# Four tiles of the first expert, ranked after six of nine attention blocks and multiplied in the stretch between attention and the first expert loop

## The chip, the cores and the metric

One Trainium2 chip; the program runs on one of its cores. TensorE (PE, with its weight loads PEld), VectorE (DVE), ScalarE (ACT), GpSimd (POOL) and SyncE (SP, which issues most DMAs) each run their own list of instructions in order and wait for one another through semaphores. The metric is the device time of one execution in microseconds; lower is better. A clock throttle grants TensorE 1.2 or 2.4 GHz; the profile gives it as a share of 2.4 (0.50 or 1.00).

## The reference

Three layers. Attention over q, k, v of shape (4, 8, 576, 64), with keys and values averaged over groups of 8. Its output, as x of 2304 rows by 512, goes through a mixture of 8 experts that takes the best expert alone, and then through a second layer in which every row goes through every expert, with Sinkhorn weights.

```python
logits = x @ w_gate                      # layer 1
e_idx = np.argmax(logits, axis=1)
for e in range(E):
    mask = e_idx == e
    h = np.maximum(x[mask] @ w1[e], 0.0)
    out[mask] = gate_w[mask, None] * eom[mask, e, None] * (h @ w2[e])
...
for e in range(E):                       # layer 2: all rows, all experts
    out += P[:, e:e + 1] * (np.maximum(x @ w1[e], 0.0) @ w2[e])
```

With the inputs of the reference, 1217 of the 2304 rows go to expert 0, 571 to expert 3, 28 to 4, 348 to 6, 140 to 7, none to the others. Of the 1536 rows of attention blocks 0 to 5, 571 go to expert 0. Both counts come from computing the reference.

## The kernel before

Matmuls are done in float16 with each operand split into a high and a low half, three products per pair (`PASSES`). A tile is 128 rows.

**Attention** (`attention`, L387) goes through nine blocks of 256 rows in the order 0 to 5, 8, 6, 7. A block has transposes of q, scores and exponentials (two halves), transposes of the exponentials, the weighing by values (`weigh`, which also gives the gate logits), and a write of the rows to the DRAM tensor `rowd`. `top1` (L468) picks the experts of finished blocks; the last call handles block 7. Meanwhile `between` loads expert 0's weights, and splits them into halves.

**Routing** (`route`, L488) needs the choices of all rows: matmuls with `ones16` count rows per expert, matmuls with `prior` and `tri` give each row its rank in the order of experts, DVE and POOL turn ranks into one-hot tiles, a matmul of these gives `idx`, the row numbers in the order of experts. POOL then issues one indirect DMA per tile of 128 sorted rows (`gather`, L798) from `rowd` into one of 8 buffers in `raw2`. `columns` (L819) transposes a gathered tile on TensorE; ACT and DVE write its halves to `xT`. `stages` and `coefs1` make the table of experts and the coefficients.

All of this up to the product of sorted tile 0 (`one`, L833: 96 matmuls of 128 columns with w1, relu and split, 24 matmuls of 512 columns with w2) is recorded by `Notes` (L1183), a planner. It lists each engine's instructions by simulating the engines with estimated costs: of what is ready on an engine, the one with the lowest number in program order goes first, `late` being added to that number. The order that it writes is fixed; on the chip an engine that reaches an instruction whose input is late waits, and everything behind it waits too.

**The expert loop** (`moe1`, L881) follows, in code with run-time branches (`tc.If` on register values). Tiles 1 to 8 of expert 0 run one by one; after each, one of the eight pieces of the next expert's weights is split (`step`). The columns of the last eight gathered tiles come after tiles 1 and 2. Then tile 9, and the other experts in turn (`item`), each splitting the weights of the expert after it during its own first two tiles. POOL meanwhile prepares weights of layer 2 (`ahead`, L964), from the moment the gather buffers are free. Layer 2 fills the rest of the span.

Of the kernel before, what the change touches and what calls it, by code (L numbers as in the profile page):

```python
# [20 lines left out]
P = 128  # L21
# [359 lines left out]

LATE = {"scores": -50, "weigh": 150, "key_layout": 100}


def attention(g):  # L387
# [282 lines left out]
def stages(g):  # L670
# [43 lines left out]
    )  # L714
    stg = g.tile([P, 5, E], F32, "stg")
    nc.vector.tensor_reduce(stg, pick, axis=AX.X, op=ALU.add)
    nc.vector.tensor_copy(g.stgi, stg[:, 0:3])
    cm = g.tile([P, 2, E, NT], F32, "cm")

    def bc(r):  # L720
# [72 lines left out]


GB = 8


def gather(g, j):  # L798

    gr = g.gat[:, j % GB]  # L800
    g.nc.gpsimd.indirect_dma_start(
        out=gr,
        out_offset=None,
        in_=g.rowd,
        in_offset=bass.IndirectOffsetOnAxis(ap=g.idx[:, j:j + 1], axis=0),
        bounds_check=N - 1,
        oob_is_err=False,
    )
    g.rows[j] = gr


def gathered(g, first, last):
    for j in range(first, last):
        columns(g, j, g.rows.pop(j))
        if j + GB < NT:
            gather(g, j + GB)


def columns(g, j, gr):  # L819
# [8 lines left out]
    hi, lo = [g.xT[:, s, :, j * P:(j + 1) * P] for s in range(2)]  # L828
    nc.scalar.copy(hi, pt)
    nc.vector.tensor_tensor(lo, pt, hi, op=ALU.subtract)  # L830

# [49 lines left out]
def moe1(g, first):  # L881
# [9 lines left out]
    xts = []
    for i in range(4):
        xt = g.xt.tile([P, 2, KC, P], F16, name=f"xt{i}")
        xts.append(xt)
# [1236 lines left out]
def attention_moe_moe(ctx: ExitStack, tc, q, k, v, wg, wo, w1, w2, wgb, w1b, w2b, out):  # L2131
# [50 lines left out]
    g.stgi = g.per.tile([P, 3, E], I32, name="stgi")  # L2182
# [141 lines left out]
```

## Time and profile before

| | |
|---|---|
| median of 3 runs | 1770.49 us (1770.3 to 1773.25) |
| profiled execution | 1781.27 us, span 1779.5 us |
| mean granted clock | 0.979 |
| PE / DVE / ACT / POOL busy in the span | 95% / 70% / 59% / 16% |
| last weighing of attention ends on PE | 119.2 us |
| first matmul of the expert loop | 162.97 us |
| first matmul of expert 3 | 262.43 us |

A busy share is an average over the stages; what a change inside one stage does is read from the instructions and waits of that stage. In the rows below, the first number of a timeline row is its start in us from the start of the span, the second its length. The helper that records instructions gives nearly all of the first 163 us the line L1293.

### The profile page before, as it was taken

What the parts mean: (1) busy time and instruction counts of PE and PEld (TensorE: products, weight loads), DVE (VectorE), ACT (ScalarE), POOL (GpSimd) and SP (SyncE); (2) the same over time, 40 slices, a digit from 0 to 9 for tenths busy, and PEclk for the clock granted to TensorE, in tenths of its full rate; (3) what the DMA queues carried; (4) which work ended last, traced back from release to release, by engine and by line L of the source; (5) the groups of instructions that cost most, each with busy time, mean ns of one, the idle gap of its engine ahead of it and who ended that gap; (6) DMA issues with size and microseconds to landing.
All of it is one profiled execution on the core that took longest, in us unless ns stands there. A gap on an engine that the chain in (4) does not pass through costs nothing. (4 is left out here: it accounts for less than half of the span.)

```text
span 1779.5 us, 40062 instructions
## 1 busy us (share of the span) xinstructions
PE 1698.0 (95%) x17079; PEld 1482.7 (83%) x17079; DVE 1239.6 (70%) x2218; ACT 1049.1 (59%) x1916; POOL 285.7 (16%) x300
## 2 busy tenths in 40 slices
PE   5868999997999999999999999999999999999997
PEld 4756776676898889889888988898899889888986
DVE  7884436667896785787588567856876786597663
ACT  4743333454577775776577557756766775576542
POOL 7833678400000000000000000000000000000011
PEclk9988999998899999999999999999999999999999
DMA  9625345357331242244134313422441242234211
GB/s 302 161 64 175 108 144 167 134 166 303 105 134 45 87 151 37 39 113 112 25 83 114 78 25 76 132 56 37 113 125 25 60 130 74 36 72 123 104 54 42
DMA packets 83170, 183.86 MB, mean 103 GB/s; under 512 B 27664, under 2 KB 35856, under 8 KB 81168
## 3 DMA queue, kind: packets, MB, share of 16 engines
q1 hardware_dynamic: 68912, 131.66, 22.3%
q0 software_dynamic: 14048, 49.29, 13.2%
q8 instruction: 145, 2.38, 0.5%
q14 instruction: 65, 0.53, 0.1%
HBM read 121.16 MB, written 59.77 MB: 102 GB/s over the span
## 5 line engine op out<-in xcount | busy, mean ns | idle before, releaser
L1797 PEld LDWEIGHTS <-w1c 128*128 128x128 f16 x6720 | 604.3, 98 | 64.6 <-issue 2.2
L1896 PEld LDWEIGHTS <-hs 128*128 128x128 f16 x6048 | 590.6, 98 | 69.8 <-issue 1.9
L1797 PE MATMUL ua<-xc,w1c 128*128 128x256 f16 (+1 forms) x3840 | 426.7, 262 | 0.8 <-DVE xc L1460 0.6
L1896 PE MATMUL da<-x,hs 128*128 128x256 f16 x2592 | 318.2, 273 | 1.4 <-ACT z L1434 0.9
L1959 POOL DMA_DIRECT2D sums<-x x54 | 45.9, 850 | 1243.8 <-ACT x L1436 1208.8
L1797 PE MATMUL uc<-xc,w1c 128*128 128x256 f16 (+1 forms) x1920 | 214.1, 263 | 0.7 <-DVE xc L1460 0.5
L1817 DVE TENSOR_TENSOR u<-u,uc 128x512 f32<-128x512 f32 x144 | 98.7, 685 | 76.6 <-ACT u L1434 61.9
L1817 DVE TENSOR_TENSOR p<-p,ub 128x512 f32<-128x512 f32 x72 | 49.3, 685 | 140.8 <-PE ub L1797 140.8
L1434 ACT COPY u<-ua 128x512 f32<-128x512 f32 x144 | 83.7, 582 | 88.3 <-PE ua L1797 87.9
L1460 DVE TENSOR_TENSOR hs<-h,hs 128x512 f16<-128x512 f32 x144 | 98.8, 686 | 43.2 <-ACT hs L1434 43.2
L1460 DVE TENSOR_TENSOR hs<-u,hs 128x512 f16<-128x512 f32 x144 | 98.9, 687 | 39.2 <-ACT hs L1434 39.2
L1436 ACT ACTIVATE u<-u 128x512 f32<-128x512 f32 x144 | 90.9, 632 | 38.6 <-DVE u L1817 38.5
L858 ACT ACTIVATE wa<-ph 128x512 f32<-128x512 f32 x42 | 25.1, 597 | 139.1 <-PE ph L853 102.8
L1797 PE MATMUL ub<-xc,w1c 128*128 128x256 f16 (+1 forms) x960 | 106.3, 262 | 0.0
L1896 PE MATMUL da<-w2r,hs 128*128 128x256 f16 x864 | 106.1, 273 | 0.0
L1896 PE MATMUL db<-x,hs 128*128 128x256 f16 x864 | 106.1, 273 | 0.0
L1896 PE MATMUL dc<-x,hs 128*128 128x256 f16 x864 | 106.1, 273 | 0.0
L1896 PE MATMUL dc<-w2r,hs 128*128 128x256 f16 x864 | 106.1, 273 | 0.0
L1434 ACT CAST hs<-p 128x512 f16<-128x512 f32 x144 | 89.3, 620 | 26.4 <-DVE p L1460 26.1
L1460 DVE TENSOR_TENSOR hs<-p,hs 128x512 f16<-128x512 f32 x144 | 98.5, 684 | 0.6 <-ACT hs L1434 0.6
L868 PEld LDWEIGHTS <-wa 128*128 128x128 f16 x504 | 48.5, 99 | 60.5 <-DVE wa L860 5.8
L1436 ACT ACTIVATE p<-p 128x512 f32<-128x512 f32 x72 | 45.2, 628 | 86.3 <-DVE p L1817 86.3
(271 smaller groups left out, 2598.4 us busy)
## 6 DMA issues: line engine op xcount, KB each, us to landing
raw<-in_moe_w_dram SPq DMA_DIRECT2D x56, 512.0 KB, 4.0
wr<-in_moe_w_dram SPq DMA_DIRECT2D x54, 512.0 KB, 4.5
sums<-x POOLq DMA_DIRECT2D x54, 512.0 KB
xc<-cspill SPq DMA_DIRECT2D x14, 1792.0 KB, 7.2
cspill<-xc SPq DMA_DIRECT2D x8, 896.0 KB, 4.4
sums<-x SPq DMA_DIRECT2D x9, 512.0 KB, 3.3
x<-sums SPq DMA_DIRECT2D x9, 512.0 KB, 3.7
wa<-in_k_dram SPq DMA_DIRECT2D x4, 1024.0 KB, 10.3
```

The source lines that it names most:

```text
L858: nc.scalar.activation(hr[:, sl], ph, AF.Relu, scale=HSC)
L868: nc.tensor.matmul(py, hs[:, a, k, :], w.w2[:, b, k, :], start=(k == 0 and t == 0), stop=(k == FC - 1 and t == 2),)
L1434: self.nc.scalar.copy(o, x)
L1436: self.nc.scalar.activation(o, x, func, scale=scale)
L1460: lambda: e.tensor_tensor(o, x, y, op=op), reads, writes, late,
L1797: nc.tensor.matmul(o, g.w1c[:, l, a, k, f * P:(f + 1) * P], g.xc[:, pr, r, b, k, :], start=(first and fi == 0 and n == 0), stop=(n == 5), ...
L1817: lambda: nc_.tensor_tensor(o_[0], o_[0], x_[0], op=ALU.add),
L1896: nc.tensor.matmul(t[x][0][:, lo], g.hs[:, sl[f // 2], l, a, f % 2, :], g.w2c[r][:, b, f, :], start=(first and n == 0), stop=(n == 11), sk ...
L1959: lambda: nc.gpsimd.dma_start(sums, x, accum_op=ALU.add), xk, [sk],
```

## The change

After block 5, `top1` is called for columns 8 to 12 too, and a new function `early_rows` ranks the rows of blocks 0 to 5 that go to expert 0. It gathers the first four tiles (512 rows) of them into the raw weight buffers wr2 and wr3. As sorted order takes rows block by block, these are sorted tiles 0 to 3, provided that at least 512 rows were found; `full` says so for each tile. `early_tiles` records the transposes and products of the four tiles with `late` at 300 and not before the last block's transposes of exponentials; their results, without coefficients, go back into wr2 and wr3 until `early_out` multiplies them by `cm`. Tile 4 takes the place that tile 0 had at the end of the planned part. The gathers run in the order 4 to 17, 0 to 3. The loop has tiles 5 to 8, with two weight pieces split after each, and the last eight gathered tiles after tiles 5 and 6. Then a new branch, over a register loaded from a fourth row of `stgi`, computes again those of tiles 0 to 3 that were not full; with these inputs it is skipped. Weights of later experts use the raw buffers shifted by two. At the start, zeros are written to 128 rows of `rowd` that the early gathers may name in their bounds.

```diff
-LATE = {"scores": -50, "weigh": 150, "key_layout": 100}
+LATE = {"scores": -50, "weigh": 150, "key_layout": 100, "early_rows": 250}
...
+    none = g.tile([64, DM], F32, "none")
+    nc.gpsimd.memset(none, 0.0)
+    for b in range(EB // 2 - 1):
+        nc.sync.dma_start(g.rowd[b * S + 512:(b + 1) * S, :], none)
...
             put(exp_transpose, ex, eT, tail)
+        g.spread = len(g.notes.tasks) - 1
...
-        if n in (3, 8, 6, 7):
-            put(top1, *{3: (0, 8), 8: (16, 18), 6: (8, 14), 7: (14, 16)}[n])
+        if n in (3, 5, 8, 6, 7):
+            put(top1, *{3: (0, 8), 5: (8, 12), 8: (16, 18), 6: (12, 14), 7: (14, 16)}[n])
+        if n == 5:
+            put(early_rows)
...
     def raw(self, i):
-        return self.g.wr[(8 * self.stage + i) % RAW]
+        return self.g.wr[(8 * self.stage + 2 * (self.stage > 0) + i) % RAW]
...
+NE = 4
+EB = 6
+ORDER = [*range(NE, NT), *range(NE)]
...
+def early_rows(g):
+    nc = g.nc
+    T = 2 * EB
+    oh = g.oh[:, 0, 0:T]
+    pc = bank2(g)
+    nc.tensor.matmul(pc[0:T, 0, 0:P], oh, g.ones16, start=True, stop=True)
+    nc.scalar.copy(cnt, pc[0:T, 0, 0:P])
+    nc.tensor.matmul(rk, cnt, g.prior[0:T, 0, 0:T + 1], start=True, stop=False)
...
+    nc.tensor.matmul(rk, g.tri, ohx, start=False, stop=True)
...
+    for t in range(T):
+        ohp = new([P, P], BF16, "eohp", 3)
+        nc.vector.tensor_scalar(
+            ohp, g.iof16, lof[:, 0, t:t + 1], 1.0, op0=ALU.is_equal, op1=ALU.mult
+        )
+        nc.tensor.matmul(
+            px[:, 0, 0:2 * NE], ohp, ohv[:, t].rearrange("p x j -> p (x j)"),
+            start=(t == 0), stop=(t == T - 1),
+        )
...
+    nc.vector.tensor_tensor(idx, high, px[:, 0, NE:2 * NE], op=ALU.add)
+    for c in range(NE):
+        gather_rows(g, g.early[c], idx[:, c:c + 1], EB // 2 * S - 64)
+
+def early_tiles(g, w):
+    for c in range(NE):
+        columns(g, g.early[c], g.xts[c])
+    for c in range(NE):
+        product(g, w, g.xts[c], lambda py, c=c: g.nc.scalar.copy(g.early[c], py), c)
+
+def early_out(g):
+    nc.vector.tensor_tensor(ce, g.cm[:, 0, 0:NE], g.full, op=ALU.mult)
+    for c in range(NE):
+        nc.vector.tensor_scalar(g.x2[:, c], g.early[c], ce[:, c:c + 1], None, op0=ALU.mult)
+        nc.vector.tensor_reduce(
+            g.am2[:, c:c + 1], g.x2[:, c], axis=AX.X, op=ALU.max, apply_absolute_value=True
+        )
...
-    for c in range(1, 9):
+    for c in range(NE + 1, 9):
         first_tiles(c)
-        if c < 3:
-            gathered(g, NT - GB * (3 - c) // 2, NT - GB * (2 - c) // 2)
-        w[1].step(c - 1)
+        i = c - NE - 1
+        if i < 2:
+            gathered(g, NT - GB * (2 - i) // 2, NT - GB * (1 - i) // 2)
+        w[1].step(2 * i, 2 * i + 1)
+    with tc.If(g.s_a[NE] > 0):
+        for c in range(NE):
+            with tc.If(g.s_a[c] > 0):
+                one(
+                    g, first, g.xT[:, :, :, c * P:(c + 1) * P], slice(c, c + 1),
+                    g.cm[:, 0, c:c + 1],
+                )
...
         attention(g)
+        g.notes.late, g.notes.after = 300, g.spread
+        early_tiles(g, first)
+        g.notes.late, g.notes.after = 0, None
...
         route(g)
...
+        early_out(g)
         gathered(g, 0, NT - GB)
-        one(g, first, g.xT[:, :, :, 0:P], slice(0, 1), g.cm[:, 0, 0:1])
+        one(
+            g, first, g.xT[:, :, :, NE * P:(NE + 1) * P], slice(NE, NE + 1),
+            g.cm[:, 0, NE:NE + 1],
+        )
```

`product` is `one` without the coefficient: the same 96 and 24 matmuls, always with the same hidden buffer, and an ACT copy of the result.

PE's instructions behind the last weighing of block 7 (`xT,x`, 81 columns), where the routing's count (`ones,oh`) and ranks (`prior,wb`) follow; before:

```order
L1293 MATMUL ab_274<-xT,x_97 128x81
L1293 LDWEIGHTS oh
L1293 MATMUL ab_277<-ones_115,oh 128x128
...
L1293 MATMUL ab_277<-ones_115,oh 16x128
L1293 LDWEIGHTS wb
L1293 MATMUL ab_275<-prior,wb 128x144
```

The same place in the changed kernel (`wr` holds the early rows, `xt_171` their columns; the lines left out are 60 matmuls with `xt_171` ahead of the count, and 24 between count and ranks):

```order
L1446 MATMUL ab_296<-xT,x_97 128x81
L1446 MATMUL ab_294<-ident,wr_71 128x128 x4
L1446 MATMUL ab_293<-ident,wr_71 128x128 x4
L1446 MATMUL ab_295<-ident,wr_72 128x128 x4
L1446 MATMUL ab_294<-ident,wr_72 128x128 x4
...
L1446 MATMUL ab_296<-xt_171,wa 128x128
L1446 LDWEIGHTS oh
L1446 MATMUL ab_293<-ones_115,oh 128x128
...
L1446 MATMUL ab_296<-xt_171,wa 128x128
L1446 LDWEIGHTS wb
L1446 MATMUL ab_295<-prior,wb 128x144
```

All 16 transposes of early rows and five eighths of the first early product with w1 now stand ahead of the count.

DVE's instructions at the last block's gate logits (`lgt`) and expert choice (`mx`, `eq`, `fi`, `oh`), on which the count waits; before:

```order
L1293 TENSOR_TENSOR raw_98<-ab_274,wa 128x640
L1293 TENSOR_REDUCE lgt<-raw_98 128x32
L1293 TENSOR_REDUCE mx<-lgt 128x2
L1293 TENSOR_TENSOR eq<-lgt,mx 128x16
L1293 TENSOR_TENSOR eq<-eq,rev 128x16
L1293 TENSOR_REDUCE fi<-eq 128x2
L1293 TENSOR_TENSOR oh<-fi,rev 128x8x2
```

And in the changed kernel:

```order
L1446 TENSOR_TENSOR xt_171<-ab_294,xt_171 128x512
...
L1446 TENSOR_TENSOR raw_98<-ab_296,wa 128x640
...
L1446 TENSOR_TENSOR xt_172<-ab_293,xt_172 128x512
L1446 TENSOR_REDUCE lgt<-raw_98 128x32
L1446 TENSOR_TENSOR xt_173<-ab_295,xt_173 128x512
L1446 TENSOR_REDUCE mx<-lgt 128x2
L1446 TENSOR_TENSOR xt_174<-ab_294,xt_174 128x512
L1446 TENSOR_TENSOR eq<-lgt,mx 128x16
L1446 TENSOR_TENSOR eq<-eq,rev 128x16
L1446 TENSOR_REDUCE fi<-eq 128x2
L1446 TENSOR_TENSOR oh<-fi,rev 128x8x2
```

The low halves of the four early tiles have been put between the last block's logits and its expert choice.

## Rows read from the trace of the kernel before

**Rows 1.** Windows: length; busy us (instructions) of PE, PEld, DVE, ACT, POOL; PEclk, DMA, GB/s.
```profile
98.00:120.00 22.00, 18.84 (x352) 16.25 (x351) 19.52 (x46) 11.54 (x13) 0.95 (x1) 0.92 0.33 74
119.00:163.00 44.00, 25.44 (x207) 18.63 (x207) 26.44 (x111) 12.55 (x19) 22.73 (x22) 0.73 0.47 155
```

**Rows 2.** Timeline of PE: start, length, what; idle before it, and its releaser.
```profile
114.62 4.55 PE L1293 MATMUL ab<-xT,x 128*128 128x81 f16 x70 [1.02 <-DVE x L1293]
122.19 0.49 PE L1293 MATMUL ab<-ones,oh 128*128 128x128 bf16 x2 [3.01 <-DVE oh L1293]
123.62 0.56 PE L1293 MATMUL ab<-prior,wb 128*128 128x144 bf16 x2
128.15 2.14 PE L1293 MATMUL ab<-wb 128*128 128x36 bf16 x18 [3.97 <-POOL wb L1293]
134.65 1.11 PE L1293 MATMUL ab<-ident,raw 128*128 128x128 f32 x4 [4.36 <-DMA raw<-rowd,idx]
138.57 2.76 PE L1293 MATMUL ab<-xT,wa 128*128 128x128 f16 x24
162.97 5.52 PE L853 MATMUL ph<-xT,wa 128*128 128x128 f16 x96 [0.94 <-DVE x L1293]
168.33 5.34 PE L868 MATMUL py<-wa 128*128 128x512 f16 x24
173.51 1.91 PE L827 MATMUL py<-ident,raw 128*128 128x128 f32 x16
```

**Rows 3.** Timeline of DVE, end of attention and routing.
```profile
112.53 0.82 DVE L1293 TENSOR_TENSOR x<-ab,wa 128x640 f32<-128x640 f32 x1
114.98 0.41 DVE L1293 SCALAR_TENSOR_TENSOR x<-ab,x 64x256 f16<-64x256 f32 x1
121.95 0.17 DVE L1293 TENSOR_TENSOR oh<-fi,rev 128x16 bf16<-128x16 f32 x1
126.11 3.91 DVE L1293 TENSOR_SCALAR wb<-iof,wb 128x128 bf16<-128x128 bf16 x16
130.54 0.17 DVE L1293 TENSOR_TENSOR idx<-wb,ab 128x18 int32<-128x18 f32 x1
136.47 0.69 DVE L1293 TENSOR_TENSOR xT<-ab,xT 128x512 f16<-128x512 f32 x1 [2.91 <-ACT xT L1293]
```

**Rows 4.** Timeline of POOL: first and fourth gather, first and last DMA of `ahead`.
```profile
131.01 1.27 POOL L1293 DMA_INDIRECT raw<-rowd,idx  x1 [1.82 <-DVE wb L1293]
135.20 1.00 POOL L1293 DMA_INDIRECT raw<-rowd,idx  x1 [0.30 <-issue]
188.01 0.58 POOL L976 DMA_DIRECT2D raw<-in_moe_w_dram  x1 [28.65 <-PE py L827]
334.95 0.68 POOL L1006 DMA_DIRECT2D w2spill<-raw  x1 [0.30 <-POOL raw L1002]
```

**Rows 5.** Windows with the granted clock (PEclk, third from the end).
```profile
138.00:141.00 3.00, 3.00 (x27) 2.93 (x26) 2.56 (x10) 0.58 (x1) 2.39 (x3) 0.50 0.61 193
141.00:144.00 3.00, 2.77 (x31) 2.56 (x29) 0.00 (x0) 0.00 (x0) 2.39 (x3) 0.79 0.65 203
```

**Rows 6.** Waits from 100 to 165 us: total, times, longest.
```profile
DVE xT L1293 <- issue: 6.7, 1, 6.7
PE ab L1293 <- issue: 3.6, 4, 2.5
```

**Rows 7.** Timeline of PE and DVE in the expert loop.
```profile
262.43 5.52 PE L853 MATMUL ph<-xt,wb 128*128 128x128 f16 x96 [0.94 <-DVE x L873]
270.73 8.14 DVE L785 SCALAR_TENSOR_TENSOR wa<-wr,wa 128x1024 f16<-128x1024 f32 x4
282.65 6.36 PE L868 MATMUL py<-wb,wa 128*128 128x512 f16 x22 [3.67 <-DVE wa L860]
346.51 7.16 PE L853 MATMUL ph<-xt,wb 128*128 128x128 f16 x96 [2.35 <-PEq L925]
355.94 4.63 DVE L785 SCALAR_TENSOR_TENSOR wa<-wr,wa 128x1024 f16<-128x1024 f32 x4 [0.27 <-ACT wa L784]
```

More of the change, by code (lines that the diff above doesn't have):

```diff
@@ L716, in stages @@
     nc.vector.tensor_reduce(stg, pick, axis=AX.X, op=ALU.add)
-    nc.vector.tensor_copy(g.stgi, stg[:, 0:3])
+    nc.vector.tensor_copy(g.stgi[:, 0:3], stg[:, 0:3])
+    again = g.tile([P, 2, E], F32, "again")
+    nc.vector.memset(again, 0.0)
+    nc.vector.tensor_scalar(
+        again[:, 1, 0:NE], g.iof[:, 0:NE], stg[:, 1, 0:1], None, op0=ALU.is_lt
+    )
+    nc.vector.tensor_scalar(
+        again[:, 0, 0:NE], g.full, -1.0, 1.0, op0=ALU.mult, op1=ALU.add
+    )
+    nc.vector.tensor_tensor(
+        again[:, 0, 0:NE], again[:, 0, 0:NE], again[:, 1, 0:NE], op=ALU.mult
+    )
+    nc.vector.tensor_reduce(
+        again[:, 0, NE:NE + 1], again[:, 0, 0:NE], axis=AX.X, op=ALU.add
+    )
+    nc.vector.tensor_copy(g.stgi[:, 3], again[:, 0])
     cm = g.tile([P, 2, E, NT], F32, "cm")
@@ L737, in registers @@
         min_val=0, max_val=NT,
+    )
+    _, g.s_a = nc.values_load_multi_w_load_instructions(
+        tab[:, 3 * E:3 * E + NE + 1], engines=[ET.PE, ET.DVE, ET.Activation, ET.SP],
+        min_val=0, max_val=NE,
     )
@@ L795, with gather_rows @@
 GB = 8
-def gather(g, j):
-    gr = g.gat[:, j % GB]
+NE = 4
+EB = 6
+ORDER = [*range(NE, NT), *range(NE)]
+def gather_rows(g, gr, idx, n=N):
     g.nc.gpsimd.indirect_dma_start(
@@ L803, in gather @@
         out_offset=None,
-        in_=g.rowd,
-        in_offset=bass.IndirectOffsetOnAxis(ap=g.idx[:, j:j + 1], axis=0),
-        bounds_check=N - 1,
+        in_=g.rowd[0:n, :],
+        in_offset=bass.IndirectOffsetOnAxis(ap=idx, axis=0),
+        bounds_check=n - 1,
         oob_is_err=False,
     )
+def gather(g, i):
+    gr = g.gat[:, i % GB]
+    j = ORDER[i]
+    gather_rows(g, gr, g.idx[:, j:j + 1])
     g.rows[j] = gr
 def gathered(g, first, last):
[L813 to L816, printed above, removed]
@@ L819, in columns @@
-def columns(g, j, gr):
+    for i in range(first, last):
+        j = ORDER[i]
+        columns(g, g.rows.pop(j), g.xT[:, :, :, j * P:(j + 1) * P])
+        if i + GB < NT:
+            gather(g, i + GB)
+def early_rows(g):
+    nc = g.nc
+    new = g.tile
+    T = 2 * EB
+    oh = g.oh[:, 0, 0:T]
+    pc = bank2(g)
+    nc.tensor.matmul(pc[0:T, 0, 0:P], oh, g.ones16, start=True, stop=True)
+    cnt = new([T, P], BF16, "ecnt")
+    nc.scalar.copy(cnt, pc[0:T, 0, 0:P])
+    rk = pc[:, 1, 0:T + 1]
+    nc.tensor.matmul(rk, cnt, g.prior[0:T, 0, 0:T + 1], start=True, stop=False)
+    ohx = new([P, T + 1], BF16, "eoh")
+    nc.vector.memset(ohx[:, T:T + 1], 0.0)
+    nc.vector.tensor_copy(ohx[:, 0:T], oh)
+    nc.tensor.matmul(rk, g.tri, ohx, start=False, stop=True)
+    full = new([P, 1], F32, "en")
+    nc.vector.tensor_copy(full, rk[:, T:T + 1])
+    nc.vector.tensor_scalar(g.full, g.iof[:, 0:NE], -float(P), full, op0=ALU.mult, op1=ALU.add)
+    nc.vector.tensor_scalar(g.full, g.full, float(P), None, op0=ALU.is_ge)
+    off = new([P, T], F32, "eoff")
+    nc.vector.tensor_scalar(off, oh, 8192.0, -8192.0, op0=ALU.mult, op1=ALU.add)
+    nc.vector.tensor_tensor(off, off, rk[:, 0:T], op=ALU.add)
+    posi, ints = new([P, T], I32, "eposi"), new([P, 2, T], I32, "eints")
+    nc.vector.tensor_copy(posi, off)
+    nc.vector.tensor_scalar(ints[:, 0], posi, 127, None, op0=ALU.bitwise_and)
+    nc.vector.tensor_scalar(ints[:, 1], posi, 7, None, op0=ALU.arith_shift_right)
+    lof = new([P, 2, T], F32, "elof")
+    nc.vector.tensor_copy(lof, ints)
+    ohj, ohv = new([P, T, NE], BF16, "eohj"), new([P, T, 2, NE], BF16, "eohv")
+    nc.vector.tensor_tensor(
+        ohj, g.iof[:, 0:NE].unsqueeze(1).to_broadcast([P, T, NE]),
+        lof[:, 1].unsqueeze(2).to_broadcast([P, T, NE]), op=ALU.is_equal,
+    )
+    nc.vector.tensor_tensor(
+        ohv, ohj.unsqueeze(2).to_broadcast([P, T, 2, NE]),
+        g.tok[:, 0:T].unsqueeze(3).to_broadcast([P, T, 2, NE]), op=ALU.mult,
+    )
+    px = bank2(g)
+    g.notes.whole = False
+    for t in range(T):
+        ohp = new([P, P], BF16, "eohp", 3)
+        nc.vector.tensor_scalar(
+            ohp, g.iof16, lof[:, 0, t:t + 1], 1.0, op0=ALU.is_equal, op1=ALU.mult
+        )
+        nc.tensor.matmul(
+            px[:, 0, 0:2 * NE], ohp, ohv[:, t].rearrange("p x j -> p (x j)"),
+            start=(t == 0), stop=(t == T - 1),
+        )
+    g.notes.whole = True
+    high, idx = new([P, NE], F32, "ehigh"), new([P, NE], I32, "eidx")
+    nc.vector.tensor_scalar(high, px[:, 0, 0:NE], float(P), None, op0=ALU.mult)
+    nc.vector.tensor_tensor(idx, high, px[:, 0, NE:2 * NE], op=ALU.add)
+    for c in range(NE):
+        gather_rows(g, g.early[c], idx[:, c:c + 1], EB // 2 * S - 64)
@@ new lines, in product @@
+def product(g, w, xt, out, half):
+    nc = g.nc
+    hr, hs = g.hid[0]
+    any2 = bank2(g)
+    for m in range(2):
+        ph = any2[:, m].rearrange("p (f n) -> p f n", n=P)
+        for mm in range(4):
+            f = 4 * m + mm
+            for k in range(KC):
+                for t, (a, b) in enumerate(PASSES):
+                    nc.tensor.matmul(
+                        ph[:, mm, :], w.w1[:, a, k, f * P:(f + 1) * P], xt[:, b, k, :],
+                        start=(k == 0 and t == 0), stop=(k == KC - 1 and t == 2),
+                    )
+        sl = slice(4 * m, 4 * m + 4)
+        nc.scalar.activation(hr[:, sl], ph, AF.Relu, scale=HSC)
+        nc.scalar.copy(hs[:, 0, sl], hr[:, sl])
+        nc.vector.tensor_tensor(hs[:, 1, sl], hr[:, sl], hs[:, 0, sl], op=ALU.subtract)
+    py = bank2(g)[:, 0]
+    g.notes.whole = False
+    for k in range(FC):
+        for t, (a, b) in enumerate(PASSES):
+            nc.tensor.matmul(
+                py, hs[:, a, k, :], w.w2[:, b, k, :],
+                start=(k == 0 and t == 0), stop=(k == FC - 1 and t == 2),
+            )
+    g.notes.whole = True
+    out(py)
@@ L820, in columns @@
+def columns(g, gr, xt):
     nc = g.nc
@@ L827, in columns @@
         nc.tensor.transpose(pt[:, k, :], gr[:, k * P:(k + 1) * P], g.ident)
-    hi, lo = [g.xT[:, s, :, j * P:(j + 1) * P] for s in range(2)]
+    hi, lo = [xt[:, s] for s in range(2)]
     nc.scalar.copy(hi, pt)
@@ L890, in moe1 @@
     ]
[L891 to L894, printed above, removed]
+    xts = g.xts
     def fetch(c, j):
@@ L2214, in attention_moe_moe @@
     first = Weights(g, 0, w1[0], w2[0])
+    g.early = [g.wr[2 + i // 2][:, i % 2 * DM:(i % 2 + 1) * DM] for i in range(NE)]
+    g.xts = []
+    for i in range(4):
+        t = g.xt.tile([P, 2, KC, P], F16, name=f"xt{i}")
+        g.xts.append(t)
+    g.full = g.per.tile([P, NE], F32, name="full")
     def between(n):
```

14 lines of the change are left out of this document (10 added, 4 removed).

## The prediction

> **What bounds the kernel now.** I read three views in turn: the busy time by windows, to find where PE is idle; the timelines of PE, DVE and POOL around that place; and the totals of waits there. PE bounds the span as a whole (95% busy), but from 119 to 163 us it works 25.4 of 44 us, at a mean clock of 0.73, so 18.6 us are idle [rows 1]. The reader should see why in the idle times of PE's rows: it waits 3.0 us for the last expert choice, 4.0 for one-hot tiles, 4.4 for the first gathered tile [rows 2]. That is the latency of a chain: last choice, count, ranks, `idx`, gather, transposes. Just before, from 98 to 120, DVE is the full engine: 19.5 of 22 us [rows 1]. And in the loop that follows PE runs without a gap: 162.97 to 168.33 for a tile's product with w1, 168.33 to 173.51 for the one with w2 [rows 2]. A tile costs 5.36 + 5.18 = 10.54 us there.
>
> So the change takes PE work from a stretch where it costs its full length, and puts it where PE waits. The question is how much longer it makes the chain, since PE and DVE take their instructions in the listed order.
>
> **What is removed.** Tiles 1 to 4 leave the loop (tile 0 was in the planned part; now tile 4 is): 4 x 10.54 = 42.2 us. Their columns stay, as the last eight gathered tiles are transposed in the loop as before. The eight pieces of weights are now split in four tiles instead of eight. That is two splits of some 1.2 us (4.63 / 4 in [rows 7]) per tile of 10.54 on ACT and DVE each, hidden. The loads ahead of these splits are the same.
>
> **What is added, as moments of the chain.** Before: last weighing ends on PE at 119.2, choice (`oh`) done at 122.1, count at 122.2, ranks done at 124.2, `idx` at 130.5, first transposes at 134.65, loop at 162.97 [rows 2, 3].
>
> *Early `idx`: 118.* DVE runs 36 more instructions before the last choice. Twelve one-hot tiles take 3.91 / 16 = 0.24 us each, 2.9; five more of `top1` and some thirteen small ones take about 0.1 each when interleaved and up to 0.2 when they wait for one another (0.17 is the length of the choice's own [rows 3]): 1.8 to 3.6, say 2.3. That is 5.2 us on the engine that is full. In the list, the early `idx` stands behind the low half of block 7's exponentials, which ended at 114.98 + 0.41 = 115.4 [rows 3], but ahead of block 6's two evacuations (0.82 us each and their small ones, [rows 3]) and logits, some 2.7. So 115.4 + 5.2 - 2.7 = 118.
>
> *Fourth early tile in: 126.3.* Before, the fourth gather started 4.66 us after `idx` (135.20 - 130.54), and a gather's transposes began 3.64 us after its start (134.65 - 131.01) [rows 2 to 4]. 118 + 8.3 = 126.3, and the transposes take under 0.7. PE's last weighing is done before that, around 122 to 123, so PE waits here for gathers.
>
> *Last choice: 129.6 instead of 122.1.* The four early low halves are listed in front of it. From the start of transposes to the end of the low half was 136.47 + 0.69 - 134.65 = 2.5 us [rows 2, 3]; 126.3 + 2.5 = 128.8, then the last four small ones, 0.8. Were the gathers early enough, it would be 122.1 + 5.2 + 4 x 0.69, less up to 2 us that DVE is idle now: 128. So the wait for gathers costs little here.
>
> *Count: 132 instead of 122.2.* In front of it are 60 matmuls of the first early tile. At 2.4 GHz they take 5.36 / 96 = 0.056 each, 3.4; at 1.2 GHz 2.76 / 24 = 0.115 each, 6.9 [rows 2]. From 127 on that gives 130.3 to 133.9. The granted clock was 0.50 at 138 to 141 with PE busy all 3 us, and rose in the next window [rows 5], so I take the middle.
>
> *Ranks done: 135. `idx`: 142.7 instead of 130.5.* Count to ranks took 2.0; 24 more early matmuls stand between (1.3 to 2.8), partly beside DVE's casts: 3. Ranks to `idx` took 6.4; DVE now also makes the two low halves of the first product's hidden layer in front, 2 x 0.69. PE's own share between (36 matmuls of 128 columns, 14 of 512: 2.0 + 3.0) lies beside DVE's chain.
>
> *First gathered tile: 146.8*, 4.1 behind `idx` as before.
>
> *Rest of the planned part.* From there, nothing but PE work: 348 matmuls at 0.056 (19.4), 96 at 5.18 / 24 = 0.216 (20.7), 40 transposes at 1.91 / 16 = 0.12 (4.8), and 0.5 for coefficients: 45.4. The first gathered tiles land 1.3 to 1.6 us apart with 1.1 to 1.8 of work between, so about 2.1 of waiting: 194.3.
>
> *Code.* In the burst of gathers the trace has DVE idle for 6.7 us and PE for 3.6 with no releaser but "issue" [rows 6]. The early gathers and the eight later ones are bursts too. I charge PE's 3.6 once: 197.9. The Trainium skill (Runtime: NRT & Kernel Launch, Instruction fetch mechanics) says that engines fetch code by a DMA queue of their own, in blocks, and that crossing a block is mostly hidden. The trace disagrees within a burst of gathers, if this is fetching; by the page the charge would be 0 and the time 3.6 lower.
>
> *Hand-over to the loop*, 0.94 as before [rows 2]: 198.8. The extra register load stands beside that wait.
>
> The planned part grows by 198.8 - 162.97 = 35.9 us; 42.2 - 35.9 = 6.3 us gained.
>
> **Later costs.** The branch that skips the four tiles: jumps at the ends of experts show 0.94, with another releaser, up to 2.35 us idle behind PE's sequencer [rows 7]. Between nothing and 2.35, I take 0.9. The same page and section says that a taken branch out of the fetched window stalls until the target is fetched, which speaks against the change; rows bound it as above.
>
> `ahead` starts when the gather buffers are free: 188 now, some 33 later then, so it ends near 368 instead of 335 [rows 4]. While it runs, a split on DVE takes 8.14 / 4 = 2.0 us instead of 1.2, and PE once waited 3.67 us for DVE in such a place [rows 7]. Parts of two more experts now come under it. From nothing to 3.7 us; I take 1. Layer 2, which reads its product, follows only behind the last expert.
>
> Hidden: the zeros written at the start (256 KB), the memset on POOL, and the last writes of `rowd`. On SP, two writes of block 8 now wait for the early gathers (to 126.3), and block 7's write is queued behind them; it lands some 4 us later, still 10 us ahead of `idx`. Without that cover it would add its delay directly.
>
> **Sum.** 6.3 - 0.9 - 1.0 = 4.4 us faster: 1781.3 to 1776.9 in the profiled execution. The median is 10.8 us below that; the same difference on it gives 1766.1 us.
>
> **Rivals.**
>
> *PE well fed (1757.5).* Were PE never idle from 119.2 on, it would do 5 x 10.54 + 56 x 0.12 + some 4 of routing = 63.4 us and, with the hand-over, reach the loop at 183.5, 20.6 later than now: 21.6 gained. DVE's 5.2 us of added work make the start later by 4 at least, so 17.6 is the limit. Half way between 21.6 and my 4.4, 13.0 gained. For it: PE has four tiles of work with no tie to routing. Against: that work is cut in portions that stand in front of and behind the chain's own instructions.
>
> *Slower, by code starvation (1775.8).* Early gathers come while DVE and PE are both dense. If DVE loses in the first burst what it lost in the later one, 6.7, in front of the last choice, and PE 3 more in the second, the 4.4 become -5.3. It decides from 7.9 us lost beyond my charge, that is when the early tiles land after 134 or PE stands still for so long. For it: [rows 6]. Against: before, the stall came only after 10 us of gathers, and the early burst is four gathers, 5 us.
>
> *Given back (1770.3).* `ahead` slows the splits of two more experts, 3.7 us, and the skipped branch costs 2.35: 6.1 instead of my 1.9 off the 6.3, leaving 0.2. For it: [rows 7]. Against: I found such a wait of PE for DVE once in the 147 us of `ahead`.
>
> *The skipped tiles run (1808).* If fewer than 512 rows were found, four products come back. 571 are found; only a fault would do this.
>
> **Chances.** Forecast, with its own range 1761 to 1769: 0.42. Well fed: 0.18. Code starvation: 0.20. Given back: 0.18. Tiles run again: 0.02. A measurement of this kernel can tell about 0.2%, 3.5 us, from no change. Faster by that needs under 1767: most of the forecast's case and the well fed one, 0.5. Slower needs over 1774: most of starvation, and the last, 0.2. The rest, 0.3, is within. Range: 1754 (17.6 gained, less the branch, rounded) to 1777 (starvation and a slow `ahead`).
>
> **What would show it.** The early gathers start near 118 and the first early transposes wait for them; `oh` for the last time near 130, the count near 132, `idx` near 143; PE nearly without idle time from 147 to the loop, which starts near 199; loop to expert 3 about 58 us instead of 99; expert 3 near 257. PE's idle time between 119 and the loop should fall from 18.6 to about 12. I am wrong if `idx` comes before 138 or after 148, if PE's waits behind "issue" grow past 7 us, or if expert 4 and 6 take longer than now.

## The result, and the profile after

The changed kernel takes 1790.89 us (median of 4 runs, 1790.25 to 1792.56), the kernel before took 1771.87 beside it: 1.0107 times as long, interval 1.0089 to 1.0124. It is 19 us slower; forecast were 1766.1, in a range to 1777.

PE's timeline in the changed kernel (start, length, what; idle before it and its releaser; DVEq or PEq is the sequencer of DVE or PE, at a branch), with the rows that answer to [rows 2] (last weighing, early transposes, count, first gathered tile, loop) and to [rows 7] (expert 3 and behind):

```profile
120.19 6.99 PE L1446 MATMUL ab<-xT,x 128*128 128x81 f16 x129 [0.55 <-DVE x L1446]
129.39 0.63 PE L1446 MATMUL ab<-ident,wr 128*128 128x128 f32 x4 [0.96 <-DMA wr<-rowd,xT]
131.92 1.21 PE L1446 MATMUL ab<-ident,wr 128*128 128x128 f32 x8 [1.91 <-DVE lgt L1446]
136.32 0.37 PE L1446 MATMUL ab<-ones,oh 128*128 128x128 bf16 x2
150.71 0.63 PE L1446 MATMUL ab<-ident,raw 128*128 128x128 f32 x4 [1.93 <-DMA raw<-rowd,idx]
202.16 3.01 PE L1001 MATMUL ph<-xT,wa 128*128 128x128 f16 x51 [0.94 <-DVE x L1446]
244.25 4.92 PE L1016 MATMUL py<-wa 128*128 128x512 f16 x22 [1.00 <-DVE wa L1008]
251.98 4.01 PE L1001 MATMUL ph<-xT,wa 128*128 128x128 f16 x69 [0.81 <-issue]
263.80 5.52 PE L1001 MATMUL ph<-xt,wb 128*128 128x128 f16 x96 [2.28 <-PEq L1081]
350.54 5.53 PE L1001 MATMUL ph<-xt,wb 128*128 128x128 f16 x96 [3.58 <-PEq L1070]
371.33 6.61 PE L1016 MATMUL py<-wb,wa 128*128 128x512 f16 x22 [3.83 <-DVE wa L1008]
422.61 3.87 PE L1742 MATMUL pt<-ident,x 128*128 128x128 f32 x16 [11.97 <-DVE x L1735]
```

The windows of the changed kernel, as in [rows 1]:

```profile
98.00:120.00 22.00, 16.41 (x235) 13.12 (x234) 18.96 (x49) 8.72 (x14) 2.57 (x2) 0.84 0.01 2
119.00:163.00 44.00, 35.77 (x447) 28.02 (x448) 32.59 (x137) 18.36 (x30) 20.92 (x21) 0.96 0.47 125
```

PE is indeed busier where it waited, 35.8 of 44 us at a clock of 0.96 instead of 25.4 at 0.73. But in the 22 us ahead of it PE works 2.4 us less than before and at 0.84 instead of 0.92, the count comes at 136.3 instead of 122.2, and PE waits longer for DVE and at branches once the loop is over.

Four moments cut each profile into stages (us): the count, the loop's start, expert 3, layer 2's first transposes.

| kernel | count at | to loop | to expert 3 | to layer 2 | span |
|---|---|---|---|---|---|
| before, first profile | 122.2 | 40.8 | 99.5 | 151.0 | 1779.5 |
| before (`b_again_2`) | 122.5 | 42.1 | 99.8 | 148.3 | 1778.1 |
| changed, first profile | 136.3 | 65.8 | 61.6 | 158.8 | 1788.2 |
| changed (`a_again`) | 139.0 | 65.5 | 61.7 | 160.8 | 1792.7 |
| changed (`a_again_2`) | 135.0 | 71.9 | 61.1 | 161.0 | 1795.6 |
| early ranking alone (`e_rank_only_2`) | 133.3 | 40.3 | 100.3 | 150.2 | 1788.7 |
| `ahead` late (`b_late_ahead`) | 122.4 | 32.9 | 100.0 | 157.4 | 1778.0 |
| `ahead` early (`b_early_ahead`) | 122.4 | 33.0 | 105.1 | 141.7 | 1767.6 |

`b_again_2`, `a_again_2` and `e_rank_only_2` ran on one chip on one occasion. There the change costs 12.5 us up to the count, 29.8 from there to the loop and 12.7 from expert 3 to layer 2, saves 38.7 in the loop, and costs 1.3 behind: 17.5 us. Each row is one execution: the count of the changed kernel alone goes from 135.0 to 139.0, so single moments are good to some 4 us.

### The profile page after: what moved, and what is told of

The parts are those of the page before. It is cut to its first block, busy times and chain, and to the rows that moved or that the text cites. A ratio compares the mean times of both kernels' runs of the same rounds, so it can differ in the third digit from the quotient of the medians.

```text
span 1788.2 us, 40218 instructions
## 1 busy us (share of the span) xinstructions
PE 1701.9 (95%) x17110; PEld 1481.9 (83%) x17110; DVE 1260.1 (70%) x2261; ACT 1051.2 (59%) x1926; POOL 293.8 (16%) x305
## 5 line engine op out<-in xcount | busy, mean ns | idle before, releaser
L1970 DVE TENSOR_TENSOR u<-u,uc 128x512 f32<-128x512 f32 x144 | 98.7, 685 | 76.3 <-ACT u L1587 61.6
L1613 DVE TENSOR_TENSOR hs<-u,hs 128x512 f16<-128x512 f32 x144 | 98.8, 686 | 39.2 <-ACT hs L1587 39.2
L1587 ACT CAST hs<-p 128x512 f16<-128x512 f32 x144 | 89.3, 620 | 26.4 <-DVE p L1613 26.1
L1587 ACT CAST hs<-h 128x512 f16<-128x512 f32 x144 | 89.3, 620 | 4.3 <-DVE h L1613 2.9
L1587 ACT CAST hs<-u 128x512 f16<-128x512 f32 x144 | 89.0, 618 | 3.1 <-DVE u L1613 1.3
```

Of the source, the lines that this page charges most:

```text
L1587: self.nc.scalar.copy(o, x)
L1613: lambda: e.tensor_tensor(o, x, y, op=op), reads, writes, late,
L1970: lambda: nc_.tensor_tensor(o_[0], o_[0], x_[0], op=ALU.add),
```

## The experiments

Ratios are to the kernel before beside each run.

**Both kernels again.** No edit.

> The kernel before, unchanged, for a second trace. The profiled execution of before took 1781.27 us against a median of 1770.49, and shows DVE idle for 6.7 us behind issue in its burst of gathers. Theory 1 (that stall is no part of a usual execution): the loop begins 8 to 11 us earlier than 162.97, near 153, no issue wait of DVE over 2 us between 100 and 165, execution near 1771. Rival (the stall is usual, and the 10.8 us lie elsewhere): the loop begins near 163 again and the stages after it are shorter.

> The kernel before, unchanged, for one more profile and its time. Theory 'the waits go with the occasion': with the count at t and the loop at t + 41, the kernel takes about 1780 us; with the loop at t + 34, about 1772 or less. Theory 'the waits are part of every execution': loop at t + 41 and the time is whatever the chip gives, 1770 too.

> The changed kernel, unchanged, on the chip of the others. If the early products themselves gain what was counted, it is well under the kernel with the early ranking alone (which was 14 us over the kernel before): 5 over the kernel before or less. If they give nothing back, as the first timing has it (19 over), it is 14 to 19 over.

> The changed kernel, unchanged. If the waits behind issue are there for the kernel before, they are in this one's early or later burst too: 1793 to 1798, ratio 1.007 to 1.009. If they are absent from both: 1791 and ratio 1.0095 to 1.011.

`b_again` took 1779.58 (before beside it: 1780.74), `b_again_2` 1781.05 (1781.61); `a_again` 1791.07, ratio 1.0095 (1.0078 to 1.0112); `a_again_2` 1797.54, 1.0091 (1.0063 to 1.0119). PE in `b_again_2`, behind the burst of gathers, where the columns are as above:

```profile
144.15 0.40 PE L1293 MATMUL ab<-xT,wa 128*128 128x128 f16 x4 [1.03 <-issue]
145.57 0.27 PE L1293 MATMUL ab<-xT,wa 128*128 128x128 f16 x2 [1.03 <-issue]
148.38 1.11 PE L1293 MATMUL ab<-ident,raw 128*128 128x128 f32 x4 [2.54 <-issue]
```

and the longest in `a_again_2`:

```profile
157.80 1.44 PE L1446 MATMUL ab<-xt,wa 128*128 128x128 f16 x12 [4.62 <-issue]
```

Such waits stand in every profile taken where the kernel before took 1780 to 1782 us, and in none of those from occasions where it took 1771 to 1774 (in `a_quiet_pool` they are waits of PE's weight loads and of ACT): without them count to loop is 33 to 34 us in kernels with the old tiles, with them 40 to 43, and in the changed kernel 65.5 to 65.8 against 71.9. So this stage is 6 to 10 us longer with them. They go with the occasion, not with the chip: one chip gave 1780 once and 1771 another time. The first profile, on which the prediction is built, has them; the times shown with it (1770.49) are those of an occasion without. The unchanged kernel before was never profiled on such an occasion, so that part is inferred from its variants.

**The early ranking, piece by piece.** `e_rank_only` keeps `early_rows` and the four gathers and drops the early products:

```diff
-        g.notes.late, g.notes.after = 300, g.spread
-        early_tiles(g, first)
...
-ORDER = [*range(NE, NT), *range(NE)]
+ORDER = [*range(NT)]
...
-    for c in range(NE + 1, 9):
+    for c in range(1, 9):
```

> The changed kernel with the early ranking and the four early gathers alone: no early transposes or products, tiles 0 to 8 in the places they had before, no second branch. Theory 1 (the chain from block 5 to idx is lengthened mainly by DVE's added ranking work): idx 5 to 7 us later than in a usual execution of before, time 5 to 7 us over before. Rival (the ranking is nearly hidden, and the early tiles' instructions in the chain make the delay): idx at most 2 us later, time within 3 us of before.

> The early ranking and the early gathers, with the tiles as before. If the early products give back what they displace, it is 5 us or more over the changed kernel; on the figures so far (1.0079 against 1.0095 on other occasions) it is 1 to 4 under it.

1796.65, ratio 1.0079 (1.0054 to 1.0103), and 1792.01, 1.0065 (1.0042 to 1.0088). On the chip of both, 10.4 of the changed kernel's 15.9 us are there without a single early product (the two intervals overlap, so the split is rough). Early tiles and their loop then gain 6.0 us up to expert 3 (33.3 later at the loop, 39.2 less in it), which the next stage takes back with 10.8.

`e_zeros_only` adds only the zeros; `e_rank_no_zeros` has the ranking with neither zeros nor gathers; `e_no_gather` has ranking and zeros. In `e_zeros_only`:

```diff
+    none = g.tile([64, DM], F32, "none")
+    nc.gpsimd.memset(none, 0.0)
+    for b in range(2):
+        nc.sync.dma_start(g.rowd[b * S + 512:(b + 1) * S, :], none)
     load(0, 0)
```

> The kernel before with nothing added but the zeros written at its start (a memset of 64 rows, two writes). In the listed order this alone lets block 1 to 5's instructions stand otherwise on DVE (the second logits' row is the 91st instead of the 84th). Theory 'ranking' (the instructions of the early ranking on the full DVE are what delays the last choice by 12.7 us): within 3 us of the kernel before, count at 122 to 124. Theory 'order' (the zeros' place moves the planner's order of the attention blocks, and that order is worse): 8 us slower or more, count at 130 or later. Theory 'burst' (four early gathers starve the engines): within 3 us.

> The early ranking with neither the zeros at the start nor the four early gathers; the tiles are as before. Theory 'ranking': 10 to 14 us slower than the kernel before, count near 133. Theory 'order': at most 5 slower, count before 128. Theory 'burst': 5 slower (the 5.2 us of DVE work that the prediction counted), count near 128.

> The early ranking with its zeros, without the four early gathers; the tiles are as before. With the gathers it was 14 us slower than the kernel before, count at 135.7. Theory 'burst': 9 slower, count near 131, no idle time behind issue on PE between 127 and 132. Theories 'ranking' and 'order': 12 to 14 slower, count 134 or later.

1777.02, 1780.47 and 1781.10 us; ratios 1.0019 (1.0008 to 1.0029), 1.0042 (1.0027 to 1.0057) and 1.0043 (1.0026 to 1.0059). Counts at 123.0, 125.5 and 131.4, with the gathers 133.3 and 135.7. Alone, the zeros don't move the count, though the kernel with them is 3.4 us slower. With the ranking the count is 5.9 later in these two profiles, but the medians differ by 0.6 us, and the profiled execution of `e_no_gather` took 7.0 us more than its median: that the zeros cost 6 us together with the ranking isn't shown. DVE's timeline in the changed kernel shows where it loses time (block 5's choice; the last row is a later one, for its usual length):

```profile
97.11 1.43 DVE L1446 TENSOR_TENSOR eq<-lgt,mx 128x32 f32<-128x32 f32 x1
99.13 1.49 DVE L1446 TENSOR_TENSOR eq<-eq,rev 128x32 f32<-128x32 f32 x1
123.05 0.17 DVE L1446 TENSOR_TENSOR eq<-lgt,mx 128x16 f32<-128x16 f32 x1
```

POOL and PE at that time, in the same timeline:

```profile
94.26 6.31 POOL L1446 TENSOR_TENSOR wa<-wr,wa 128x1024 f16<-128x1024 f32 x3
101.81 0.30 PE L1446 MATMUL ab<-xT,x 128*128 128x144 f16 x1 [2.27 <-DVE x L1446]
```

and the window behind (PEclk is third from the end):

```profile
100.00:105.00 5.00, 3.19 (x23) 3.06 (x24) 3.81 (x8) 1.28 (x2) 0.57 (x1) 0.50 0.00 0
```

The two comparisons of block 5's new choice end at 98.54 and 100.62, just where POOL's second and third of three instructions (6.31 / 3 = 2.10 each) end: 98.47 and 100.57. They lost some 2.5 us; DVE's next evacuation is late, PE waits 2.27 us, and its granted clock is 0.50 in the window behind. In `e_rank_no_zeros` the first of them took 1.09, the second 0.18. The early gathers may add to it: in `e_rank_only_2` DVE waits at 128.69, while PE's last weighing trickles behind "issue":

```profile
128.69 0.17 DVE L1419 TENSOR_SCALAR wa<-ab 128x8 f32<-128x8 f32 x1 [3.21 <-remote]
```

How the 12.5 us are shared I can't say closer: the parts don't add. `e_rank_no_zeros` and `e_no_gather` also took 155.9 and 155.6 us from expert 3 to layer 2, with `ahead` where it was (75 and 76 us ahead of expert 3), which nothing here explains. So that stage also varies by some 7 us for a reason other than `ahead`'s start.

`e_after_q` is the changed kernel with rows of `q` copied instead of the zeros, which gives blocks 0 to 5 nearly their old order:

```diff
-    none = g.tile([64, DM], F32, "none")
-    nc.gpsimd.memset(none, 0.0)
     for b in range(EB // 2 - 1):
-        nc.sync.dma_start(g.rowd[b * S + 512:(b + 1) * S, :], none)
+        nc.sync.dma_start(
+            g.rowd[b * S + 512:(b + 1) * S, :].rearrange("p (h d) -> p h d", h=H),
+            g.q[b, :, 512:576, :].rearrange("h p d -> p h d"),
+        )
```

> The changed kernel with other finite rows copied into the scratch rows by one transfer each (from q, in DRAM) in place of the memset and the write of zeros; the rows are never picked. This leaves the listed order of blocks 0 to 5 nearly as in the kernel before (84th, not 92nd row for the second logits). Theory 'order and DVE work both': the ranking alone cost 2.6 us at the count without the zeros and 8.3 with them, so the count comes 5 us earlier (131) and the time falls by 4 to 6 against the changed kernel, still 10 over the kernel before. Theory 'burst of early gathers alone': the time stays within 2 us of the changed kernel.

> The changed kernel with rows copied in place of the memset and write of zeros, which leaves the listed order of blocks 0 to 5 nearly as before. Theory 'order': 4 to 6 us under the changed kernel on the same chip, count 4 us earlier. Theory 'the order matters only for one profile': same within 2 us.

1794.75, ratio 1.0072 (1.0046 to 1.0098), and 1793.56, 1.0078 (1.0047 to 1.0109); beside `a_again_2` 4.0 us less, the expected size, but the intervals overlap. And the count came at 135.9 and 137.1, not 4 us earlier, though the comparisons took 0.18 to 0.19 again: the mechanism expected failed, so the two slow comparisons are not shown to delay the count, and 2.4 of the 4 us lie between expert 3 and layer 2.

**Place of the early tiles.** `e_route_first` lists them behind the ranking of all tokens (`after` = `idx`).

> The changed kernel with the early tiles' work listed behind the ranking of all tokens (its idx) instead of behind the last block's exponentials; everything else as changed. If the early tiles stand in the chain's way (the prediction's 'last choice' and 'count' steps: four low halves, 60 and 24 matmuls, two low halves of the hidden layer), count comes 3 to 4 us earlier, idx 4 to 6 earlier and the time falls by 2 to 5 against the changed kernel. If the delay is all made before (early ranking, order of the blocks, early gathers), count stays at 135 to 139 and PE waits the 10 us of the ranking's latency with nothing to do: 5 us slower than the changed kernel or more.

1813.57, ratio 1.0170 (1.0144 to 1.0195). The count came at 133.8, but PE then worked 26.4 of 46 us, as the window shows:

```profile
119.00:165.00 46.00, 26.37 (x231) 19.63 (x232) 31.20 (x137) 14.02 (x23) 24.86 (x25) 0.60 0.50 139
```

So the early work does fill PE's waits, and its place in front of the chain is the better one.

**POOL's arithmetic beside the experts.** `b_quiet_pool` and `a_quiet_pool` leave POOL's arithmetic out of `ahead`, before and changed (a memset stands in its place): layer 2's first expert gets no proper weights. `ahead`'s transfers, no longer waiting for the arithmetic, then end ahead of expert 3 too, so the runs take its traffic out of the stage as well.

> The kernel before with POOL's arithmetic in ahead left out (its DMAs stay, so layer 2's first expert gets wrong weights). Theory 1 (POOL's arithmetic slows DVE's splits, and the changed kernel has more of it beside experts 3, 4 and 6): about 4 us faster than before, the wait of 3.7 us near 282 gone. Rival (nothing of it matters): same time as before.

> The changed kernel with POOL's arithmetic in ahead left out, as in the run on the kernel before. Theory 1: about 12 us faster than the changed kernel, some 1779, so that the distance to the equally quiet before shrinks from 19 to about 11; the time from expert 3 to layer 2 falls from 158.8 to about 148. Rival (the overlap costs nothing, the waits come from loads of weights or from code): time stays at 1790 and the waits of PE for DVE remain.

1771.90, ratio 0.9948 (0.9930 to 0.9967), and 1790.98, 1.0051 (1.0036 to 1.0066). From expert 3 to layer 2 they took 141.8 and 145.5 us, against 148 to 151 and 159 to 161, so in that stage the two kernels are 3.7 us apart instead of 12.7. In time the expectation failed: the distance was to shrink to about 11 us and is 19.1, no less than with the arithmetic (16 to 19). In the changed one's profile the loop started at 210.95 and took 67.2 (206.87 and 61.1 in `a_again_2`), with waits of 4.0 and 2.3 us at the skipped branch, and that takes 10 of the 15 us back. The later start comes ahead of `ahead`'s first transfer (236.0), so the missing arithmetic isn't its cause; why the loop is longer is open. This pair shows the contention in the stage, and not how much of the whole difference is due to it.

DVE's forms of these stages, 262 to 413 us of the kernel before (columns: line, engine, operation, names, shapes, count; busy us, mean ns; idle before):

```profile
L785 DVE SCALAR_TENSOR_TENSOR wa<-wr,wa 128x1024 f16<-128x1024 f32 x16 | 25.3, 1622 | 1.1 <-ACT wa L784 1.1
L785 DVE SCALAR_TENSOR_TENSOR wb<-wr,wb 128x1024 f16<-128x1024 f32 x16 | 20.8, 1340 | 1.2 <-ACT wb L784 1.2
L860 DVE TENSOR_TENSOR wa<-wa 128x512 f16<-128x512 f32 x24 | 21.1, 880 | 28.4 <-ACT wa L859 25.4 <-ACTq L925 3.0
L873 DVE SCALAR_TENSOR_TENSOR x<-py,cm,x 128x512 f32 x12 | 9.0, 747 | 14.6 <-PE py L868 14.6
```

in the changed kernel:

```profile
L813 DVE SCALAR_TENSOR_TENSOR wa<-wr,wa 128x1024 f16<-128x1024 f32 x16 | 31.5, 2007 | 0.3 <-ACT wa L812 0.3
L813 DVE SCALAR_TENSOR_TENSOR wb<-wr,wb 128x1024 f16<-128x1024 f32 x16 | 22.6, 1455 | 1.1 <-ACT wb L812 1.1
L1008 DVE TENSOR_TENSOR wa<-wa 128x512 f16<-128x512 f32 x24 | 26.1, 1087 | 18.1 <-ACT wa L1007 16.4 <-ACTq L1070 1.7
L1021 DVE SCALAR_TENSOR_TENSOR x<-py,cm,x 128x512 f32 x12 | 8.9, 744 | 15.2 <-PE py L1016 15.2
```

and in `b_quiet_pool`:

```profile
L785 DVE SCALAR_TENSOR_TENSOR wa<-wr,wa 128x1024 f16<-128x1024 f32 x16 | 18.9, 1222 | 2.1 <-ACT wa L784 2.1
L785 DVE SCALAR_TENSOR_TENSOR wb<-wr,wb 128x1024 f16<-128x1024 f32 x16 | 18.9, 1222 | 2.1 <-ACT wb L784 2.1
L860 DVE TENSOR_TENSOR wa<-wa 128x512 f16<-128x512 f32 x24 | 16.6, 692 | 30.8 <-ACT wa L859 26.9 <-ACTq L925 4.0
L873 DVE SCALAR_TENSOR_TENSOR x<-py,cm,x 128x512 f32 x12 | 9.0, 749 | 15.2 <-PE py L868 15.2
```

A split into `wa` (both operands in SBUF) takes 1222 ns beside a quiet POOL, 1622 before and 2007 now, one into `wb` 1222, 1340 and 1455; a hidden layer's low half 692, 880 and 1087; the sum with one operand in PSUM keeps its 747. The Trainium skill (SBUF — State Buffer, Who interferes with whom) says that a DVE instruction with two SBUF inputs contends with a POOL instruction that reads SBUF, and calls the port pair that they share an exclusive lock. These rows and the two comparisons agree.

How this reaches PE is seen in its waits from expert 3 to layer 2 (us in all, times, longest) and in the window of that stage (columns as in [rows 1]). In `b_again_2`:

```profile
PE ph L853 <- PEq L925: 4.2, 3, 2.0
PE py L868 <- DVE wa L860: 3.3, 2, 2.3
264.40:412.71 148.31, 129.39 (x1440) 92.37 (x1441) 93.23 (x105) 59.66 (x80) 59.03 (x56) 0.97 0.48 157
```

in `a_again_2`:

```profile
PE py L1016 <- DVE wa L1008: 10.1, 7, 3.0
PE ph L1001 <- PEq L1070: 7.0, 3, 4.7
267.93:428.92 160.99, 131.45 (x1441) 93.37 (x1441) 102.80 (x105) 59.66 (x80) 92.29 (x88) 0.95 0.50 168
```

PE waits 6.8 us more for low halves and 2.8 more at branches, and its own work takes 2.1 more at a clock of 0.95 instead of 0.97: 11.7 of the 12.7 us. The last 1.0 is the wait ahead of layer 2 (12.4 instead of 11.4).

`b_psum_lo` makes the low half from PSUM, with powers of two moved into weights and rows:

```diff
-        nc.scalar.activation(hr[:, sl], ph, AF.Relu, scale=HSC)
-        nc.scalar.copy(hs[:, 0, sl], hr[:, sl])
-        nc.vector.tensor_tensor(hs[:, 1, sl], hr[:, sl], hs[:, 0, sl], op=ALU.subtract)
+        nc.scalar.activation(hs[:, 0, sl], ph, AF.Relu)
+        nc.vector.scalar_tensor_tensor(
+            hs[:, 1, sl], ph, 0.0, hs[:, 0, sl], op0=ALU.max, op1=ALU.subtract
+        )
```

> The kernel before with powers of two moved so that the low half of an expert's hidden layer is made on DVE from PSUM and one SBUF operand instead of two SBUF operands, and ScalarE makes the high half in one instruction instead of two. Theory 'lock' (DVE waits for POOL's running instruction when both its operands are in SBUF; 692 ns became 880 and 1087 for this form, while forms with one SBUF operand kept their 747 and 686): the form keeps its length while POOL computes, PE's waits of 2.6 and 0.5 us for it shrink, 2 to 5 us faster. If POOL slows DVE in any form: the form still grows to 0.85 or more beside POOL, and the time is the same within 2 us.

The form in that kernel, same stretch:

```profile
L862 DVE SCALAR_TENSOR_TENSOR wa<-ph,wa 128x512 f16<-128x512 f32 x24 | 16.6, 691 | 26.9 <-ACT wa L861 22.9 <-ACTq L929 4.0
```

1781.27, ratio 1.0003 (0.9992 to 1.0015): the mechanism held (691 beside a busy POOL), the gain of 2 to 5 us didn't come. PE's waits from expert 3 to layer 2 show where it went: those for the low halves are nearly gone, but PE now waits at the branches, behind DVE's sequencer, for longer.

```profile
PE ph L856 <- DVEq L929: 9.2, 3, 5.9
PE py L872 <- DVE wa L862: 0.4, 1, 0.4
```

`b_late_ahead` and `b_early_ahead` move `ahead`, by the turns in which the last eight gathered tiles are transposed. The first has them behind the turns 5 and 6, the second ahead of the first turn; the edit of the first:

```diff
-        if c < 3:
-            gathered(g, NT - GB * (3 - c) // 2, NT - GB * (2 - c) // 2)
+        if c in (5, 6):
+            gathered(g, NT - GB * (7 - c) // 2, NT - GB * (6 - c) // 2)
```

> The kernel before with the last eight gathered tiles transposed in the loop's turns 5 and 6 instead of 1 and 2; ahead, which needs their buffers, then starts 42 us later, as it does in the changed kernel. Theory 'late ahead' (its arithmetic on POOL holds up more of DVE's splits and low halves in the stages of many experts): the loop's start and the 100 us of the loop stay, expert 3 to layer 2 grows by 8 to 12 us, and the time by as much. Theory of the prediction's 'later costs' step: 0 to 3.7 us.

> The kernel before with the last eight gathered tiles transposed ahead of the loop's first turn instead of behind its first and second; ahead then starts near 170 instead of 188. Theory 'the price follows ahead's start' (9.2 us for 34 us later, 0.27 per us): expert 3 to layer 2 shrinks by 4 to 5 us; PE waits at most 1.5 us for the eight tiles' casts (0.69 each on DVE against 0.5 of transposes); 3 to 4 us faster, ratio 0.998. Rival 'the first 70 us of ahead lie beside the first expert's tiles anyway and only its end counts': as ahead's end moves by the same, no difference to the first theory there; but if DVE's waits stay with the same experts, same within 1.5 us.

Late: 1781.88, ratio 1.0055 (1.0036 to 1.0074), 9.2 us; `ahead` starts at 222.5, 33 us ahead of expert 3 (before 74, changed 37), and the split takes what it takes in the changed kernel:

```profile
L785 DVE SCALAR_TENSOR_TENSOR wa<-wr,wa 128x1024 f16<-128x1024 f32 x16 | 31.5, 2009 | 0.8 <-ACT wa L784 0.8
```

PE's waits there are near those of the changed kernel too:

```profile
PE py L868 <- DVE wa L860: 8.1, 6, 2.2
PE ph L853 <- PEq L925: 7.3, 3, 3.9
```

Early: 1769.94, ratio 1.0002 (0.9989 to 1.0016). `ahead` starts at 163.8, 97 us ahead of expert 3, and the stage shrinks to 141.7, more than expected. That is what it took beside a quiet POOL, though low halves still took 869 ns: PE waited for none of them. But loop to expert 3 grows by 5, with this wait for the tiles' casts in it, so the 3 to 4 us expected are not won:

```profile
160.03 3.42 PE L827 MATMUL py<-ident,raw 128*128 128x128 f32 x16 [2.69 <-DVE xT L830]
```

**The waits behind "issue".** `b_spaced` issues four gathers first, not eight, each further one behind a tile's transposes.

> The kernel before with four gathers issued behind idx instead of eight, each further one behind the transposes of a tile four earlier. Theory 'burst' (PE's 6.5 us of waits behind issue at 141 to 150, which some executions have and others don't, come from eight gathers back to back): no such waits, loop at 34 us behind the count, and 5 us faster where the kernel before shows them, same where it doesn't. If the waits have another cause: they are there as before, time the same or up to 3 slower for tiles that come later.

1780.64, ratio 1.0003 (0.9989 to 1.0017); seven such waits of PE, 4.9 us in all, stood at 141 to 149 as before. Eight gathers back to back aren't their cause; what is stays open.

## Why the prediction was wrong

The step that failed is "Later costs", where the prediction took 1 us for the later `ahead`, "from nothing to 3.7 us". Its mechanism is right and its size was off: 12.7 us between the two kernels on one chip; `b_late_ahead`, with the products in their old place, shows 9.2 in the time. I priced one wait of PE for DVE; PE's waits for low halves went from two, 3.3 us, to seven, 10.1, and those at branches from 4.2 to 7.0. `ahead` also ended later than I said, at 382.9 instead of 368: it started at 227.2 instead of 221, and POOL needed 156 us for it instead of 147. And the early tiles themselves caused it, as I read these runs: the four products taken out of the loop were the cover beside which POOL could work without being felt. The rival "Given back" named this and allowed 3.7 for it.

The other terms, against `b_again_2` and `a_again_2`:

- *Early `idx`: 118, last choice: 129.6, count: 132.* In the first profile 123.1, 135.1, 136.3. The early `idx` is 5 us late already, so the step on DVE's added work has the first of these errors. Up to the count the change costs 12.5 us instead of 9.8. Why is open: the 5.2 us left out that two of the new instructions meet POOL's (2.5 us), that PE waits behind them at a clock of 0.50, and the early gathers' burst, but `e_after_q` is without the first and its count is no earlier.
- *Count to loop:* 66.8 forecast. 65.8 and 65.5 without waits behind "issue", 71.9 with them; against before, 29.8 more instead of 26.0. In the first profile the gathered tile came 4.0 behind `idx` (4.1 said), and from there to the loop took 51.5 (52.0 said, the code charge in it).
- *Loop:* 38.7 saved instead of 41.3; PE's waits at the skipped branch were 1.5 and 1.4 us instead of 0.9 in all.
- *Base.* The median belonged to an occasion without the waits behind "issue" that the profile had. I noted the 10.8 us between them and didn't ask what they were. For the difference this matters little (16 us on an occasion with the waits, 17.5 and 19 without), as the changed kernel has them too; "Slower, by code starvation" is thus not what made it slower, though PE does wait in the first burst.

Together 2.7 + 3.8 + 2.6 + 11.7, and 1.3 behind layer 2's start: 22 us between the forecast's -4.4 and 17.5. So "Later costs" is the largest term and about half of the error: with 11.7 us less there, the change would still have cost 5.8 us.

Right were: the chain of moments in its order, the place ahead of the chain (`e_route_first`), and the filling of PE's idle time: from 119 us to the loop PE is busy 72.6 of 83.2 us in the first profile, so 10.5 are idle instead of 18.6, where about 12 was forecast. The net gain up to the experts was not: expert 3 was to start 5.4 us earlier and starts 3.5 later (264.4 and 267.9). The 6.0 us that the early products gain are against a kernel that has already paid for the early ranking; that they are near the 5.4 is chance. Of the prediction's signs of being wrong, `idx` behind 148 appeared in one of three profiles (146.7, 149.1, 145.3).

## What to carry to other kernels

Before you take work out of a stretch, list what else runs beside it: the first expert's products were the cover for POOL's arithmetic, and without them it cost more than was gained. Price contention by all of PE's waits over the whole stage, with the neighbour early, late and quiet, not by the one wait that it happened to cause; the mean of a form tells that there is contention, and not its price (880 ns of the low half before, 869 in `b_early_ahead` with no wait of PE for one, 691 in `b_psum_lo` with nothing won). And where a profiled execution and the median differ by more than the change is worth, find the rows that make the difference first.

## What was not expected of the hardware

- DVE instructions of 0.2 us took 1.4, ending with POOL's running instruction. DVE was full there, PE then waited 2.27 us and its clock was 0.50 in the window behind; that this delayed the count isn't shown.
- A DVE form freed of the contention (691 ns instead of 839 to 880) bought nothing: PE's waits moved from the low halves (3.3 us, now 0.4) to the branches.
- PE's waits behind "issue" come on some occasions and not on others, on the same chip, and the same kernel takes 1771 us on the ones and 1781 on the others.
